# Seven block products for half of an up layer in batch 0's second unit, with its sums in used-up weight columns

## The chip, the cores and the metric

The kernel runs on one core of a Trainium2 chip. The metric is the device time of one execution in microseconds (us), here the median of three runs. One further execution was taken by the hardware profiler; all rows of the trace are from that one.

## The reference

For each of 8 batches, linear attention over 8 heads of 1024 positions and 64 features, and then a maxout layer over the 512 joined features:

```python
k_proj = np.einsum('ks,bhsd->bhkd', E, k)          # 64 rows in place of 1024
v_proj = np.einsum('ks,bhsd->bhkd', F, v)
scores = scale * np.matmul(q, k_proj.transpose(0, 1, 3, 2))
attn = softmax(scores)                              # with its maximum taken off, and 1e-09 added to the sum
x = np.matmul(attn, v_proj)                         # then joined to [8192, 512]
h1 = x @ w1                                         # w1, w2: [512, 1024]
h2 = x @ w2
g = np.maximum(h1, h2)
out = g @ w_out                                     # w_out: [1024, 512]
```

## The kernel before

**The algebra.** With wd = w1 - w2 the layer is max(h1, h2) = relu(x @ wd) + x @ w2, so out = relu(x @ wd) @ w_out + x @ m with m = w2 @ w_out. The first product is called the up layer here, the second sum the down layer. wd_sb and m_sb are made once, on the chip, while batch 0 runs: wd_sb by VectorE in four steps of 256 columns each (`step_wd_rows`, called `wd[0]` to `wd[3]`, two instructions on line 549 each), w2 transposed by TensorE and copied out by ScalarE in four steps (`step_w2t`, lines 557 and 563), and m by `m_steps` (line 634).

**The units.** Each batch has two units of 512 positions; there are 16 units. From batch 1 on, the up layer of a unit is done by block products (`up_steps`): operands are cut in two by two blocks, and seven products of blocks, with sums of blocks made on VectorE before and after, stand in for eight. It is done in two halves d of the feature columns; half d = 1 has the column blocks 2, 3, 6 and 7 of 128 columns each. One product is four matmuls of 256 columns (line 746). The pieces are p1, p2, p6, p5, p7, p3, p4: p1, p6, p5 and p7 are copied out of PSUM by ScalarE (`keep`, line 720), p2 and p3 are added to kept ones by VectorE (line 761), which then takes the relu in place (line 764), and p4 goes out by ScalarE with the relu (line 807). The sums of x that the products need are s_x (`sums_x`, line 706), those of wd are t_w (`step_tw`, line 597); those of g for the down layer are s_g.

**Batch 0** has no such up layer. It takes direct matmuls: `up_slots` gives u0[fb] and u1[fb], for the first and the second unit, fb = 0 to 7, each a block of 128 feature columns by four matmuls of 512 columns (line 525) and a relu out of PSUM, by ScalarE (line 534) except for fb = 3, which VectorE does (line 536). u0[0], u0[1], u1[0] and u1[1] are done in two parts each.

**The order** is written out by hand. `slots` is a list of pieces that all issue in this order; `at_slot` hangs more steps behind a piece. Each engine runs its own instructions in the order in which they were issued, and waits by semaphores for the others. In the stage that the change is in, the list is:

```python
    slots = [
        (0, lambda: u0[0](r0=2)), (1, lambda: u0[1](r0=2)), (None, lambda: loads(1, "v", "q", "k")),
        (None, lambda: step_w2t(256, True)),
        (2, lambda: u1[0](r0=2)), (3, lambda: u1[1](r0=2)),
        (None, wd[1]), (4, u0[2]), (5, u0[3]),
        (None, wd[2]), (6, u1[2]), (7, u1[3]), (None, wt[2]), (None, wt[3]), (8, u0[4]), (9, u0[5]), (None, wd[3]),
        (10, u1[4]), (11, u1[5]), (12, u0[6]), (13, u0[7]),
        (14, u1[6]), (15, u1[7]),
        *((16 + n, x) for n, x in enumerate(m_steps())),
    ]
```

`wt[2]` and `wt[3]` are the transposes of w2's columns from 512 and from 768 on. Behind the pieces of m come those of the down layer of unit 0, `("P", 0, p, i)`.

**Memory.** PSUM has four banks `mm0` to `mm3`, used in turn or by number (`mm_bank`), and two pairs of banks `att` (`att_banks`). s_x, s_g and t_w lie in `big` tiles, which had held E and F (box 0), w1 (box 1), w2 (box 2) and transposed w2 (box 3); `open_box` takes such a tile anew.

Of the kernel before, what the change touches and what calls it, by code (L numbers as in the profile page):

```python
# [19 lines left out]
def kernel(  # L20
# [310 lines left out]
    Z = D // 2  # L331
# [184 lines left out]
    def up_slots(t, j):  # L516
        t["gt", j] = gt = gpool.tile([128, NFB, HALF], FP16, tag="gt", name="gt_sb")
        for fb in range(NFB):
            def up(fb=fb, r0=0, r1=NDC):
                if r0 == 0:  # L520
                    t["up", j, fb] = mm_bank(n=None if r1 == NDC else first_banks[j][fb])
                h_ps = t["up", j, fb]
                order = range(NDC) if fb < 2 else (0, 2, 1, 3)
                for r in order[r0:r1]:
                    nc.tensor.matmul(  # L525
                        out=h_ps,
                        lhsT=wd_sb[:, r, fb * 128 : (fb + 1) * 128],
                        rhs=t["xt"][:, r, :, j * W : (j + 1) * W],
                        start=(r == 0), stop=(r == NDC - 1),
                    )  # L530
                if r1 < NDC:
                    return
                if fb != 3:
                    nc.scalar.activation(out=gt[:, fb, :], in_=h_ps, func=ACTF.Relu)
                else:
                    nc.vector.tensor_scalar_max(gt[:, fb, :], h_ps, 0.0)
            yield up
# [78 lines left out]
    def m_steps():  # L616
# [2 lines left out]

        def product(k, name, n):  # L620
            if n is not None:
                st[name] = mm_bank(n=n)
            bank = st[name]
            Bb = lambda h, c: wo_sb[:, h * NG : (h + 1) * NG, c * CH : (c + 1) * CH]
            T = lambda i: T_sb[:, i, 0:NG, :]
            a, w_ = {
                1: lambda: (m_blk(0, 0), Bb(0, 0)), 2: lambda: (m_blk(0, 1), Bb(1, 0)),
                3: lambda: (m_sums[3], Bb(1, 1)), 4: lambda: (m_blk(1, 1), T(3)),
                5: lambda: (m_sums[0], T(0)), 6: lambda: (m_sums[1], T(1)),
                7: lambda: (m_sums[2], T(2)),  # L630
            }[k]()
            for i in range(2):
                for c in range(NG):
                    nc.tensor.matmul(  # L634
                        out=bank[:, i * CH : (i + 1) * CH],
                        lhsT=a[:, c, i * 128 : (i + 1) * 128],
                        rhs=w_[:, c, :],
                        start=(n is not None and i == 0 and c == 0),
                        stop=(c == NG - 1), skip_group_check=True,
                    )  # L640
            return bank
# [5 lines left out]
            nc.vector.tensor_tensor(out=block(j, c), in0=two(x), in1=two(y), op=ALU.add)  # L647

        def p1():
            st["s1"] = keep("pu", product(1, "X", 2))  # L650

        def p2():
            add(0, 0, product(2, "Y", 3), st["s1"])

        def p6():
            st["u1"] = keep("pu", product(6, "X", None))

        def p5():
            st["s5"] = keep("pu", product(5, "Z", 1))

        def p7():
            st["u2"] = keep("pu", product(7, "X", None))
# [17 lines left out]

    def t_w(i):
        return box[0].rearrange("q (s n m) -> q s n m", s=4, n=NX)[:, i]

    def step_tw(i):
        sub4(
            [t_w(i) for i in range(4)],
            lambda h, c: wd_sb[:, h * NX : (h + 1) * NX, c * HALF : (c + 1) * HALF], (i,),
        )

    def x_blk(u, j, h):  # L690
# [25 lines left out]
        step_s(u, g_blk, s_g, which)  # L716

    def keep(tag, bank, copy=nc.scalar.copy):
        x = ppool.tile([128, 512], FP32, tag=tag, bufs={"pu": 3, "pd": 4}[tag], name="p_sb")
        copy(out=x, in_=bank)  # L720
        return x

    def new_gt(u):
        u["gt"] = gpool.tile([128, NFB, HALF], FP16, tag="gt", name="gt_sb")


    def up_steps(u):
        for d in range(2):
            st = {}
            xbank, ybank = (2, 3) if d == 0 else (3, 2)  # L730

            def product(k, name, n, st=st, d=d):
                if n is not None:
# [21 lines left out]
            two = lambda ap: ap.rearrange("q (m n) -> q m n", m=2)  # L755

            def c_blk(j, c, d=d):
                return u["gt"][:, c * NG + 2 * d : c * NG + 2 * d + 2, j * W : (j + 1) * W]

            def add(j, c, x, y, c_blk=c_blk):  # L760
                nc.vector.tensor_tensor(out=c_blk(j, c), in0=two(x), in1=two(y), op=ALU.add)  # L761
# [1 line left out]
            def relu(ap):  # L763
                nc.vector.tensor_scalar_max(ap, ap, 0.0)  # L764

            def p1(st=st, product=product, xbank=xbank, d=d):
                if d == 0:
                    new_gt(u)
                st["s1"] = keep("pu", product(1, "X", xbank))
# [5 lines left out]
            def p6(st=st, product=product):  # L775
                st["u1"] = keep("pu", product(6, "X", None))

            def p5(st=st, product=product, ybank=ybank):
                st["s5"] = keep("pu", product(5, "Z", ybank))

            def p7(st=st, product=product):
                st["u2"] = keep("pu", product(7, "X", None))
# [230 lines left out]
    def loads(b, *names):  # L1013
        for n in names:
# [12 lines left out]
            elif b_ < B:  # L1027
                load_all(tiles[b_], b_, n, {"k": k, "v": v, "q": q}[n])

    slots = [  # L1030
        (0, lambda: u0[0](r0=2)), (1, lambda: u0[1](r0=2)), (None, lambda: loads(1, "v", "q", "k")),
        (None, lambda: step_w2t(256, True)),
        (2, lambda: u1[0](r0=2)), (3, lambda: u1[1](r0=2)),
        (None, wd[1]), (4, u0[2]), (5, u0[3]),
        (None, wd[2]), (6, u1[2]), (7, u1[3]), (None, wt[2]), (None, wt[3]), (8, u0[4]), (9, u0[5]), (None, wd[3]),
        (10, u1[4]), (11, u1[5]), (12, u0[6]), (13, u0[7]),
        (14, u1[6]), (15, u1[7]),
        *((16 + n, x) for n, x in enumerate(m_steps())),
    ]
    slots = [((0, n), x) for n, x in slots]  # L1040

# [27 lines left out]
        steps.setdefault(key, []).append(lambda: s(*a))  # L1069


    for key, s_, *a in (
        *((10 + i // 2, sums_m, i) for i in range(4)), *((12 + i, step_t, 0, (i,)) for i in range(4)),
        (11, open_box, 1), (11, sums_x, U[0, 0], (0, 1)),
        (15, open_box, 0, 2), (17, sums_x, U[0, 0], (2, 3)),
        (18, sums_g, U[0, 0], (0, 1)), (19, sums_g, U[0, 0], (2, 3)), (22, open_box, 3),
    ):
        at_slot((0, key), s_, *a)


    t = tiles[1]
    at_slot((0, 22), new_attn, t)
    at_slot((0, 22), lambda: turn.__setitem__(slice(None), [2, 3]))
    for n, x in enumerate((
        "", "", "", "", "", "kv", "", "kpt", "qt00 qt10", "", "sc00 sc10", "qt01",
        "qt11 dn00 in00 dn10 in10", "", "", "at00 AT10 sc01",
    )):
        key = ("P", n // 15, (n - 1) // 2 % 7, (n - 1) % 2) if n else (0, 22)
        for name in x.split():
            if name[0] == "k":  # L1090
                if name == "kpt":
# [272 lines left out]
```

## Time and profile before

| | |
|---|---|
| median of 3 runs | 319.89 us (319.75 to 320.46) |
| the profiled execution | 320.29 us |
| its span, first to last instruction | 318.5 us |
| granted TensorE clock | 1.0 |
| TensorE (PE) busy | 311.8 us, 98%, 3922 matmuls |
| VectorE (DVE) busy | 241.1 us, 76% |
| ScalarE (ACT) busy | 206.0 us, 65% |
| GpSimd (POOL) busy | 41.4 us, 13% |

In the rows of the trace the first number is the start in us from the span's start and the second the length; then come the engine, the line of the kernel, the operation, out<-in and the count. PEld is TensorE's weight load. A bracket tells how long the engine was idle before the row and what ended that. Where rows are grouped, the numbers behind the bar are the busy time in us and the mean length of one in ns. Matmuls are pipelined: the length of one is longer than the distance from its start to the next one's.

### The profile page before, as it was taken

To read this page: it belongs to the slowest core of one execution; us is meant where nothing else is said; L and a number is where in the kernel's file an instruction comes from. 1 tells how busy PE (TensorE), PEld (TensorE's weight loads), DVE (VectorE), ACT (ScalarE), POOL (GpSimd) and SP (SyncE) were. 2 spreads that over 40 slices of the span, in tenths; PEclk is the share of its full clock that TensorE was granted. 3 is DMA by queue.
4 is the path that set the end of the run, shared out by engine and by line. 5 is a ranking of instruction groups with operands and counts; after the bars stand their busy time and mean duration, and the time that the engine had idled before them with its cause. 6 is when DMAs were issued, how large, how long until landed. Compare 5 with 4: busy or idle time off the path is not lost.

```text
span 318.5 us, 9309 instructions
## 1 busy us (share of the span) xinstructions
PE 311.8 (98%) x3922; PEld 253.8 (80%) x3922; DVE 241.1 (76%) x442; ACT 206.0 (65%) x373; POOL 41.4 (13%) x63
## 2 busy tenths in 40 slices
PE   7999999999999999999999999999999999999996
PEld 3565588888887888788887888788887888888885
DVE  2366889887969696896969696996969696969883
ACT  2386742777776777477776777477776777765541
POOL 8259102004000300012000400030000000000000
PEclk9999999999999999999999999999999999999999
DMA  7999999999989999799999999989979131313124
GB/s 179 206 202 197 207 207 201 207 156 141 204 163 183 171 209 245 208 188 147 225 229 219 169 199 245 221 155 174 230 153 217 42 101 36 102 35 102 36 99 136
DMA packets 76684, 53.71 MB, mean 169 GB/s; under 512 B 29664, under 2 KB 76128, under 8 KB 76640
## 3 DMA queue, kind: packets, MB, share of 16 engines
q0 software_dynamic: 30688, 28.05, 56.0%
q1 hardware_dynamic: 45664, 24.85, 33.1%
q8 instruction: 31, 0.51, 0.6%
q10 hardware_dynamic: 288, 0.20, 0.2%
q14 instruction: 13, 0.11, 0.1%
HBM read 57.15 MB, written 16.78 MB: 232 GB/s over the span
## 4 chain that ended last, share of the span: by engine, by line
PE 95%; DMA 3%; ACT 1%; DVE 1%; issue 0%; POOLq 0%
PE mm_ps L838 47%; PE mm_ps L746 27%; PE mm_ps L525 4%; PE mm_ps L195 4%; PE att_ps L352 4%; PE mm_ps L340 2%; DMA k_sb<-in_k_dram 2%; PE mm_ps L634 2%; PE att_ps L237 1%; PE mm_ps L311 1%; PE mm_ps L153 1%; DMA out_dram<-o_sb 1%; PE att_ps L340 0%; DVE qt_sb L316 0%; ACT ld_sb L388 0%
## 5 line engine op out<-in xcount | busy, mean ns | idle before, releaser
L720 ACT COPY p_sb<-mm_ps 128x512 f32<-128x512 f32 x179 | 101.7, 592 | 49.2 <-PE mm_ps L746 27.3
L838 PEld LDWEIGHTS <-big 128*128 128x128 f16 x768 | 73.5, 98 | 11.8 <-issue 3.6
L838 PE MATMUL mm_ps<-T_sb,big 128*128 128x256 f16 x576 | 76.9, 273 | 0.0
L761 DVE TENSOR_TENSOR gt_sb<-mm_ps,p_sb 128x512 f16<-128x512 f32 x56 | 38.5, 688 | 43.0 <-PE mm_ps L746 41.6
L746 PE MATMUL mm_ps<-big,big 128*128 128x256 f16 x336 | 50.4, 273 | 0.0
L746 PEld LDWEIGHTS <-big 128*128 128x128 f16 x448 | 43.8, 98 | 5.1
L838 PE MATMUL mm_ps<-wo_sb,gt_sb 128*128 128x256 f16 x256 | 42.6, 273 | 0.0
L838 PEld LDWEIGHTS <-gt_sb 128*128 128x128 f16 x376 | 35.7, 98 | 6.7 <-issue 2.7
L469 ACT ACTIVATE ex_sb<-mm_ps 128x512 f16<-128x512 f32 x50 | 27.2, 597 | 18.0 <-PE mm_ps L340 12.3
L746 PEld LDWEIGHTS <-wd_sb 128*128 128x128 f16 x336 | 32.9, 98 | 3.8
L746 PE MATMUL mm_ps<-xt_sb,wd_sb 128*128 128x256 f16 x224 | 32.8, 273 | 0.0
L499 DVE TENSOR_TENSOR xt_sb<-att_ps,ld_sb 128x1024 f16<-128x1024 f32 x26 | 31.7, 1219 | 0.2
L303 POOL COPY junk<-qt_sb 1x1 f16<-1x1 f16 x6 | 2.6, 432 | 172.3 <-DMA qt_sb<-q_sb 172.3
L838 PE MATMUL mm_ps<-m_sb,xt_sb 128*128 128x256 f16 x128 | 24.4, 273 | 0.0
L869 DVE TENSOR_TENSOR o_sb<-mm_ps,p_sb 128x512 f32<-128x512 f32 x32 | 21.9, 683 | 2.8 <-ACT p_sb L898 2.0
L764 DVE TENSOR_SCALAR gt_sb<-gt_sb 128x512 f16<-128x512 f16 (+1 forms) x60 | 20.9, 348 | 2.1
L706 DVE TENSOR_TENSOR big<-gt_sb 128x1024 f16<-128x1024 f16 x32 | 21.9, 683 | 0.0
L838 PE MATMUL mm_ps<-wo_sb,big 128*128 128x256 f16 x128 | 21.5, 273 | 0.0
L807 ACT ACTIVATE gt_sb<-mm_ps 128x512 f16<-128x512 f32 x28 | 16.8, 601 | 5.7 <-PE mm_ps L746 5.7
L838 PE MATMUL mm_ps<-T_sb,gt_sb 128*128 128x256 f16 x120 | 20.3, 273 | 0.0
L838 PEld LDWEIGHTS <-xt_sb 128*128 128x128 f16 x188 | 18.3, 98 | 2.3 <-issue 0.2
L761 DVE TENSOR_TENSOR gt_sb<-p_sb 128x512 f16<-128x512 f32 x28 | 19.1, 682 | 0.6 <-ACT p_sb L720 0.6
(121 smaller groups left out, 434.8 us busy)
## 6 DMA issues: line engine op xcount, KB each, us to landing
out_dram<-o_sb SPq DMA_DIRECT2D x62, 256.0 KB
k_sb<-in_k_dram POOLq DMA_DIRECT2D x7, 1024.0 KB, 9.7
v_sb<-in_v_dram POOLq DMA_DIRECT2D x7, 1024.0 KB, 15.4
q_sb<-in_q_dram POOLq DMA_DIRECT2D x5, 1024.0 KB, 22.8
q_sb<-in_q_dram POOLq DMA_DIRECT2D x6, 512.0 KB, 15.9
big<-in_moe_w_dram POOLq DMA_DIRECT2D x12, 128.0 KB, 6.4
v_sb<-in_v_dram POOLq DMA_DIRECT2D x4, 256.0 KB, 14.0
wo_sb<-in_moe_w_out_dram POOLq DMA_DIRECT2D x1, 1024.0 KB, 10.4
```

What stands on the lines that cost most here:

```text
L195: nc.tensor.matmul(out=kv_ps[r * KP : (r + 1) * KP, h * D : (h + nh) * D], lhsT=eft[i][:, c, :], rhs=t[w][:, h0 + h : h0 + h + nh, c, :], ...
L352: nc.tensor.matmul(out=dst(r ^ (hh % 2))[hh * Z : (hh + 1) * Z, :], lhsT=weights(rows, hh), rhs=ex[rows, hh % 2, hh // 2 * W : (hh // 2 + ...
L469: nc.scalar.activation(out=t["ex", g, j][:, e, :], in_=banks[e], func=ACTF.Exp, scale=scale)
L499: nc.vector.tensor_tensor(out=x_out(t, g, j).rearrange("q z o n -> q o z n"), in0=at_ps.rearrange("q o (z n) -> q o z n", z=2), in1=ld[:, ...
L706: nc.vector.tensor_tensor(out=S(i), in0=S(0) if x is None else x, in1=y(), op=op)
L720: copy(out=x, in_=bank)
L746: nc.tensor.matmul(out=bank[:, m * W : (m + 1) * W], lhsT=w_[:, n_, (2 * d + m) * 128 : (2 * d + m + 1) * 128], rhs=a[:, n_, :], start=(n ...
L761: nc.vector.tensor_tensor(out=c_blk(j, c), in0=two(x), in1=two(y), op=ALU.add)
L764: nc.vector.tensor_scalar_max(ap, ap, 0.0)
L807: nc.scalar.activation(out=out, in_=in_, func=ACTF.Relu)
L838: nc.tensor.matmul(out=bank[i][:, 0:CH] if two_banks else bank[:, i * CH : (i + 1) * CH], lhsT=a(c)[:, i * 128 : (i + 1) * 128], rhs=w_(c) ...
L869: nc.vector.tensor_tensor(out=o_sb, in0=two(x), in1=two(y), op=ALU.add)
```

## The change

Four direct pieces of batch 0's second unit, u1[2], u1[3], u1[6] and u1[7], are replaced by the d = 1 half of `up_steps`, S1, S2, S6, S5, S7, S3, S4 in the order of issue. The rest of batch 0's up layer stays direct. With it:

- The four sums of xt for unit 1 (`sums_x(U[0, 1], ...)`) are made early, behind wd[1], and before S1. t_w is made in two halves: d = 1 behind wd[3], d = 0 later, during unit 0's down layer.
- s_x of units 0 and 1 (modulo 3) and s_g lie in columns of w1_sb and w2_sb that have been used up, and no longer in boxes of their own.
- All of m's seven products (M1 to M4) go into the `att` banks, and u0 and u1 take turns in `mm0` and `mm1` (by fb modulo 2); S1 to S4 have `mm2` and `mm3`. The transposes of w2 from column 512 and 768 on go into `att` banks too, at other places in the order.
- M2's sum with the kept M1 (`M_add`) is issued later, behind M6 and two sums of g.
- S3's two sums and the relu behind them (`rest`) are held until unit 0's down layer has begun. S1, S6, S5 and S7 are kept in the pool `soft`.

```diff
-                    t["up", j, fb] = mm_bank(n=None if r1 == NDC else first_banks[j][fb])
+                    t["up", j, fb] = mm_bank(n=first_banks[j][fb] if r1 < NDC else fb % 2)
...
             if n is not None:
-                st[name] = mm_bank(n=n)
+                if n % 2 == 0:
+                    st["att"] = att_banks()
+                st[name] = st["att"][:, n % 2, :]
...
         def p2():
-            add(0, 0, product(2, "Y", 3), st["s1"])
+            st["c0"] = product(2, "Y", 1)
...
-        return [p1, p2, p6, p5, p7, p3, p4]
+        return [p1, p2, p6, p5, p7, p3, p4, lambda: add(0, 0, st["c0"], st["s1"])]
 
     def s_g(i):
-        return box[2].rearrange("q (s n m) -> q s n m", s=4, n=NG)[:, i]
+        return (w1_sb, w2_sb)[i // 2][:, :, HALF + i % 2 * CH : HALF + (i % 2 + 1) * CH]
 
     def s_x(i, u):
         n = u["n"] % 3
-        half = box[1 if n < 2 else 3].rearrange("q (h s n m) -> q h s n m", h=2, s=4, n=NX)
-        return half[:, n % 2, i]
+        if n == 2:
+            return box[3].rearrange("q (h s n m) -> q h s n m", h=2, s=4, n=NX)[:, 0, i]
+        r = i % 2 * NX
+        return (w1_sb, w2_sb)[n][:, r : r + NX, i // 2 * CH : (i // 2 + 1) * CH]
...
-    def step_tw(i):
+    def step_tw(i, d):
+        f0 = d * CH
...
-    def up_steps(u):
-        for d in range(2):
+    def up_steps(u, halves=range(2)):
+        for d in halves:
             st = {}
-            xbank, ybank = (2, 3) if d == 0 else (3, 2)
+            tag = "soft" if u["b"] == 0 else "pu"
+            xbank, ybank = (2, 3) if d == 0 or u["b"] == 0 else (3, 2)
...
                 bank = product(3, "Z", None)
+                if u["b"] == 0:
+                    def rest(u=u, st=st, d=d, bank=bank):
+                        add(0, 1, bank, st["u1"])
+                        add(1, 1, st["u2"], st["s5"])
+                        relu(up_gt(u)[:, NG + 2 * d : NG + 2 * d + 2, :])
+
+                    u["rest"] = rest
+                    return
...
+    open_box(0)
+    S1, S2, S6, S5, S7, S3, S4 = up_steps(U[0, 1], (1,))
+    M1, M2, M6, M5, M7, M3, M4, M_add = m_steps()
     slots = [
-        (0, lambda: u0[0](r0=2)), (1, lambda: u0[1](r0=2)), (None, lambda: loads(1, "v", "q", "k")),
...
+        lambda: u0[0](r0=2), lambda: u0[1](r0=2), lambda: loads(1, "v", "q", "k"),
+        lambda: step_w2t(256, True),
+        lambda: u1[0](r0=2), lambda: u1[1](r0=2), wd[1], lambda: sums_x(U[0, 1], range(4)),
+        u0[2], u0[3], S1, S2, lambda: step_w2t(512, True), wd[2],
+        u0[4], lambda: step_w2t(768, True), u0[5], wd[3], lambda: [step_tw(i, 1) for i in range(4)] and None,
+        u1[4], S6, u1[5], S5, u0[6], S7, u0[7],
+        lambda: [sums_m(i) for i in range(4)] and None, S3, S4,
+        lambda: step_t(0, (0, 1)), M1, lambda: step_t(0, (2, 3)), M2, lambda: sums_x(U[0, 0], (0, 1)),
+        M6, lambda: sums_g(U[0, 0], (0, 1)), M_add, M5, lambda: sums_g(U[0, 0], (2, 3)), M7, M3, M4,
+        lambda: (open_box(3), new_attn(tiles[1]), turn.__setitem__(slice(None), [2, 3])) and None,
     ]
...
-        if n in (2, 3):
-            for i in range(2):
-                at_slot(key, step_tw, 2 * (n - 2) + i)
+        if n == 2:
+            at_slot(key, sums_x, U[0, 0], (2, 3))
+        if n == 3:
+            at_slot(key, lambda: U[0, 1]["rest"]())
         if 6 <= n < 10:
-            at_slot(key, sums_x, U[0, 1], ((2, 0, 1, 3)[n - 6],))
+            at_slot(key, step_tw, n - 6, 0)
```

In the changed kernel the lines stand lower: the products of `m_steps` are on line 636, `keep` copies on 728, `up_steps` multiplies on 758, adds on 773, takes its relu in place on 776 and p4's on 827, the sums s_x and s_g are on 711, and the down layer multiplies on 858 (838 before).

More of the change, by code (lines that the diff above doesn't have):

```diff
@@ L718, in keep, with up_gt @@
     def keep(tag, bank, copy=nc.scalar.copy):
-        x = ppool.tile([128, 512], FP32, tag=tag, bufs={"pu": 3, "pd": 4}[tag], name="p_sb")
+        if tag == "soft":
+            x = soft.tile([128, 512], FP32, tag=tag, name="p_sb")
+        else:
+            x = ppool.tile([128, 512], FP32, tag=tag, bufs={"pu": 3, "pd": 4}[tag], name="p_sb")
         copy(out=x, in_=bank)
         return x
+    def up_gt(u):
+        return u["t"]["gt", u["o"]] if u["b"] == 0 else u["gt"]
     def new_gt(u):
         u["gt"] = gpool.tile([128, NFB, HALF], FP16, tag="gt", name="gt_sb")
-    def up_steps(u):
-        for d in range(2):
+    def up_steps(u, halves=range(2)):
+        for d in halves:
             st = {}
-            xbank, ybank = (2, 3) if d == 0 else (3, 2)
+            tag = "soft" if u["b"] == 0 else "pu"
+            xbank, ybank = (2, 3) if d == 0 or u["b"] == 0 else (3, 2)
             def product(k, name, n, st=st, d=d):
@@ L757, in c_blk @@
             def c_blk(j, c, d=d):
[L758 removed]
+                return up_gt(u)[:, c * NG + 2 * d : c * NG + 2 * d + 2, j * W : (j + 1) * W]
             def add(j, c, x, y, c_blk=c_blk):
@@ L1087 @@
     )):
-        key = ("P", n // 15, (n - 1) // 2 % 7, (n - 1) % 2) if n else (0, 22)
+        key = ("P", n // 15, (n - 1) // 2 % 7, (n - 1) % 2)
         for name in x.split():
```

42 lines of the change are left out of this document (13 added, 29 removed).

## The prediction

> **What bounds the kernel now.** I read the page's busy times and its chain first, then TensorE's list of waits, then busy times by window, and last the timelines of TensorE, VectorE and ScalarE from 24 to 46 us, where the change lies.
>
> ```profile
> span 318.5 us, 9309 instructions
> PE 311.8 (98%) x3922; PEld 253.8 (80%) x3922; DVE 241.1 (76%) x442; ACT 206.0 (65%) x373; POOL 41.4 (13%) x63
> PE 95%; DMA 3%; ACT 1%; DVE 1%; issue 0%; POOLq 0%
> ```
>
> TensorE works 311.8 of 318.5 us, and the chain that ends last is TensorE for 95% of its length. Where the other 6.7 us lie is told by its waits, longest first, and by one window:
>
> ```profile
> PE mm_ps L153 <- DVE ones L146: 1.5, 1, 1.5
> PE mm_ps L1196 <- DMA out_dram<-o_sb: 1.2, 1, 1.2
> PE mm_ps L195 <- DMA k_sb<-in_k_dram: 1.0, 1, 1.0
> PE att_ps L352 <- ACT vp_sb L207: 0.5, 1, 0.5
> ...
> 24.00:64.00 40.00, 40.00 (x464) 28.86 (x462) 32.38 (x63) 23.42 (x39) 10.54 (x14) 1.00 1.29 204
> ```
>
> The list has seven waits in all, and by their lines they belong to the start, to the attention of batch 0 and to the last store. In the window the columns are length, then busy time of PE, weight loads, DVE, ACT and POOL: TensorE is busy for 40.00 of 40.00 us. So in the stage that the change rewrites TensorE has no slack. A microsecond of its work taken out is worth a microsecond; a microsecond for which it is made to wait costs one, and nothing later gives it back, as no wait follows until the last store.
>
> **The work taken out of TensorE.** Its timeline through the stage, and the length of one matmul:
>
> ```profile
> 27.31 4.48 PE L525 MATMUL mm_ps<-xt_sb,wd_sb 128*128 128x512 f16 x20
> 31.63 1.06 PE L557 MATMUL mm_ps<-ident,big 128*128 128x128 f16 x16
> 32.52 7.07 PE L525 MATMUL mm_ps<-xt_sb,wd_sb 128*128 128x512 f16 x32
> 39.43 1.91 PE L634 MATMUL mm_ps<-wo_sb,big 128*128 128x256 f16 x16
> 41.17 2.78 PE L634 MATMUL mm_ps<-T_sb,p_sb 128*128 128x256 f16 x24
> L525 PE MATMUL mm_ps<-xt_sb,wd_sb 128*128 128x512 f16 x64 | 14.5, 379 | 0.0
> L746 PE MATMUL mm_ps<-big,big 128*128 128x256 f16 x336 | 50.4, 273 | 0.0
> ```
>
> Start to start gives the price in the stream: (39.43 - 32.52) / 32 = 0.216 us for 512 columns, (41.17 - 39.43) / 16 = 0.109 for 256, (32.52 - 31.63) / 16 = 0.0556 for a transpose. The change drops four pieces of the second unit (u1[2], u1[3], u1[6], u1[7]: 16 matmuls of 512 columns, 3.45 us) and adds seven products of four matmuls of 256 columns (28 x 0.109 = 3.05 us). That is a gain of **0.40 us** and no more: 0.13% of the time, too small to be told from no change here (about 0.2%, or 0.64 us, is what can be told). Whatever the rest of the change does, its price is weighed against these 0.40 us.
>
> **The wait that is put in.** The new order on TensorE from u0[3] on is: u0[3], S1, S2, eight transposes of w2, u0[4]. u0[4] reads the columns of wd_sb that step wd[2] makes on VectorE. VectorE runs its queue in order, and there wd[2] now stands behind two new instructions: S2's sum with the kept S1 (line 773), and a relu of that sum (line 776). Before, wd[2] stood directly behind the relu of u0[3]. The rows of before:
>
> ```profile
> 27.22 0.42 DVE L549 TENSOR_TENSOR wd_sb<-big,big 128x512 f16<-128x512 f16 x1 [0.25 <-DMA big<-in_moe_w_dram]
> 30.10 0.69 DVE L536 TENSOR_SCALAR gt_sb<-mm_ps 128x512 f16<-128x512 f32 x1 [2.46 <-PE mm_ps L525]
> 30.71 0.84 DVE L549 TENSOR_TENSOR wd_sb<-big,big 128x512 f16<-128x512 f16 x2
> 31.83 0.69 DVE L536 TENSOR_SCALAR gt_sb<-mm_ps 128x512 f16<-128x512 f32 x1 [0.28 <-PE mm_ps L525]
> 32.44 0.75 DVE L549 TENSOR_TENSOR wd_sb<-big,big 128x512 f16<-128x512 f16 x2
> 34.23 0.69 DVE L706 TENSOR_TENSOR p_sb<-big 128x1024 f16<-128x1024 f16 x1 [1.05 <-ACT big L563]
> 28.97 1.62 ACT L534 ACTIVATE gt_sb<-mm_ps 128x512 f16<-128x512 f32 x3
> 32.27 1.93 ACT L563 COPY big<-mm_ps 128x1024 f16<-128x1024 f16 x2 [0.71 <-PE mm_ps L557]
> 40.50 0.58 ACT L720 COPY p_sb<-mm_ps 128x512 f32<-128x512 f32 x1 [0.28 <-PE mm_ps L634]
> ```
>
> Before, wd[2] was done at 30.71 + 0.84 = 31.55, and u0[4] started at 32.52: a cover of one microsecond. Now the two sides run like this.
>
> TensorE: u0[3]'s last matmul still starts at 27.31 + 11 x 0.216 = 29.69 and ends 0.38 later, at 30.07 (VectorE starts on it at 30.10, so 0.03 to 0.04 after an end). S1 starts at 29.90 and ends at 29.90 + 3 x 0.109 + 0.27 = 30.50. S2 starts at 30.34 and ends at 30.94. The transposes start at 30.77, and after 8 x 0.0556 TensorE is free for u0[4] at **31.22**.
>
> ScalarE keeps S1: behind its relus, which end at 30.59 and overlap the next start a little, and 0.04 after S1's end, so from 30.54; 0.58 long, done at 31.12. VectorE follows ScalarE by 0.03 (32.27 + 1.93 = 34.20, and its row starts at 34.23), so the sum starts at 31.15. What follows such a sum, in a later up layer of the same form:
>
> ```profile
> 83.84 0.69 DVE L761 TENSOR_TENSOR gt_sb<-mm_ps,p_sb 128x512 f16<-128x512 f32 x1 [0.42 <-PE mm_ps L746]
> 84.56 0.29 DVE L764 TENSOR_SCALAR gt_sb<-gt_sb 128x512 f16<-128x512 f16 x1
> 84.77 0.68 DVE L869 TENSOR_TENSOR o_sb<-mm_ps,p_sb 128x512 f32<-128x512 f32 x1
> 12.11 1.29 DVE L316 COPY qt_sb<-mm_ps 128x1024 f16<-128x1024 f16 x2 [0.90 <-PE mm_ps L311]
> 13.45 0.41 PE L340 MATMUL att_ps<-qt_sb,kpt_sb 64*32 64x256 f16 x16 [0.16 <-DVE qt_sb L316]
> ```
>
> The relu starts 0.72 after the sum (31.87), and the next independent instruction 0.21 after that: wd[2]'s first half at 32.08, 0.42 long (line 549's rows), done at 32.50. TensorE follows VectorE by 0.05 (12.11 + 1.29 = 13.40, then 13.45). So u0[4] starts at 32.55 and not at 31.22: a stall of **1.33 us**. wd[2]'s second half comes 0.33 later (two take 0.75, one 0.42), at 32.83, and is wanted at 32.55 + 2 x 0.216 = 32.98, so it adds nothing.
>
> From there to the first matmul of w2 @ w_out TensorE has 24 x 0.216 + 20 x 0.109 + 8 x 0.0556 = 7.81 us: 40.36 against 39.43 before, **0.93 us later**. That is the 1.33 less the 0.40.
>
> Bounds. Below: if ScalarE were no hindrance, the sum would start at 30.98, as S2 itself ends at 30.94, and the net is +0.75. Above: if wd[2] waited for the relu's end (0.29 and not 0.21), and TensorE followed VectorE as late as it did here,
>
> ```profile
> 23.37 0.48 DVE L541 TENSOR_TENSOR wd_sb<-big,big 128x256 f16<-128x256 f16 x2
> L541 DVE TENSOR_TENSOR wd_sb<-big,big 128x256 f16<-128x256 f16 x2 | 0.5, 283 | 0.0
> 23.82 1.41 PEld L525 LDWEIGHTS <-wd_sb 128*128 128x128 f16 x8 [0.21 <-DVE wd_sb L541]
> ```
>
> where the first piece of wd_sb was done at 23.37 + 0.28 = 23.65 and its weights were loaded at 23.82, 0.17 later and not 0.05, the net is +1.13. I take 0.93, as each of its steps has a row of the same engines and shape.
>
> **What is moved and costs nothing.** The four sums of xt go into VectorE's idle time ahead of u0[3]'s relu: from 27.67, four of about 0.42 with two that depend on each other, done by 29.3, against 30.10. Should they run on, they would delay that relu and with it all of the above. The shared operands t_w for S6 come after wd[3]: about 33.6 to 35.2, S6 wants them at 32.55 + 4 x 0.216 + 0.45 + 8 x 0.216 = 35.6, and it is the second of the four, done at 34.5, that it reads. The four sums for w2 @ w_out wait for the last copy of transposed w2 (about 35.1) and end near 37.8; then the T products wait for w_out:
>
> ```profile
> 27.03 0.88 POOL L143 DMA_DIRECT2D wo_sb<-in_moe_w_out_dram  x1
> wo_sb<-in_moe_w_out_dram POOLq DMA_DIRECT2D x1, 1024.0 KB, 10.4
> ```
>
> It lands at 27.03 + 10.4 = 37.4, three microseconds ahead of its use by M1 at 40.4. The second of the T products is done near 39.2 and is read by M6 at 42.1. The other banks for w2 @ w_out have been free since the last transposes were copied. M_add, put behind two sums, is done near 43.1; its block is read by the first piece of the down layer only after 46.5. The held sums and relu of S3 take the places on VectorE in which t_w was made before, and t_w's other half takes the places of the sums of xt; they are read units later. No DMA moves in its queue, on POOL or SP. The slot that issues loads waits for TensorE at the same point, so batch 2's loads slip by the same 0.9 us as their readers.
>
> **The rivals.** *The gain is kept.* Slower turns into not slower if wd[2] is done by 31.17, so that TensorE meets it: then 319.89 - 0.40 = 319.49. For it: only that the chain's end-to-start gaps are worked out and not seen. Against it: S2 must end before its sum starts, and 30.98 + 0.72 + 0.21 + 0.42 is 32.33 with nothing else in the way. Chance 0.08.
>
> *The delay is absorbed.* If a later wait that the profile doesn't show had slack, the time would stay near 319.9. The full window and the list of waits speak against it. Chance 0.10.
>
> *The banks.* u0 and u1 now take turns in two banks, where four were used, so u1[4] needs ScalarE's relu of u0[4] to be over, and u1[5] that of u0[5], behind a 1 us copy of transposed w2. By the rows above these relus end near 34.2 and 35.6, wanted at 34.7 and 36.0: margins of 0.5 and 0.4. If ScalarE ran later by a whole relu, 0.6 each, the stall would grow by some 0.1 to 0.2 each; if it fell behind by a whole copy (1.0), by 0.5 each, thus 321.8. Chance 0.06.
>
> *The clock.* At its start TensorE runs at half speed, and a short stop later doesn't bring that back:
>
> ```profile
> 1.47 3.43 PE L153 MATMUL mm_ps<-ones 128*128 128x512 f16 x8 [1.47 <-DVE ones L146]
> 8.57 1.03 PE L195 MATMUL mm_ps<-k_sb,eft 128*64 128x256 f16 x8 [1.04 <-DMA k_sb<-in_k_dram]
> ```
>
> The first eight matmuls of 512 columns come every (3.43 - 0.38) / 7 = 0.44 us, twice the 0.216 of later. After the stop of 1.04 us at 8.57 eight of 256 columns come every (1.03 - 0.27) / 7 = 0.109, which is full speed. The new stall is 1.33, a little longer than any stop shown but the first. If it did throw TensorE back for as long as the first stretch, eight matmuls would lose 0.21 each, 1.7 us: 322.5. Chance 0.02. The Trainium skill, "TensorE: Matmul & The Clock Gate", Part 1, says that the clock halves after one idle window of about 3.4 us and needs as long a busy one to return; by that rule a stall of 1.33 us is free of it, and the row at 8.57 agrees as far as 1.04 us goes.
>
> **How the numbers follow.** The profiled execution took 320.29 us for its span of 318.5; the median of the three runs is 319.89 (319.75 to 320.46). The difference, +0.93, goes on the median: 320.82, which I give as 320.8 (the span would be 319.4). The forecast has chance 0.74; its own range, with its bounds and the 0.3 us or so by which runs differ, is 320.4 to 321.3. The range down to 320.2 and up to 321.6 takes in some of the absorbed case and of the banks, and leaves out under 2 in 10. Slower by over 0.2% (above 320.53): 0.68 of the forecast, and the banks and the clock, 0.76. Within 0.2%: 0.06 of the forecast, 0.10 of absorption, 0.05 of the kept gain, 0.21. Faster by over 0.2%: TensorE's work allows only 0.40 us, so it is what runs may scatter, 0.03.
>
> **What would show it.** In the profile of the changed kernel: a wait of TensorE on line 525 put down to VectorE's wd_sb (line 549), 1.1 to 1.5 us long, near 31.2 to 32.6; ahead of it on VectorE the rows of lines 773, 776 and 549 in that order, the first starting near 31.15 and released by ScalarE; the first matmul of line 636 near 40.4; no other TensorE wait up to 315 us. The prediction is wrong if TensorE passes from line 557 to line 525 there without a wait, if line 549's third instruction is done before 31.5, or if the matmuls behind the stall come slower than one in 0.216 us.

## The result, and the profile after

| | before | changed |
|---|---|---|
| median, 5 runs each | 319.75 us (319.63 to 320.46) | 323.32 us (323.14 to 323.65) |
| the profiled execution, its span | 320.29, 318.5 | 323.32, 321.5 |
| granted TensorE clock | 1.0 | 1.0 |

By the medians the changed kernel takes 3.57 us more; the ratio over all runs is 1.0108, with a 95% interval of 1.0096 to 1.0119. Slower was forecast, but 320.8, with a range up to 321.6.

The head of the page of the changed kernel, and its window from 24 to 64 us (length, then busy time of PE, weight loads, DVE, ACT, POOL):

```profile
span 321.5 us, 9348 instructions
PE 312.0 (97%) x3934; PEld 255.0 (79%) x3934; DVE 244.3 (76%) x450; ACT 207.0 (64%) x375; POOL 39.7 (12%) x63
...
24.00:64.00 40.00, 37.56 (x421) 28.18 (x420) 32.30 (x67) 23.27 (x39) 10.30 (x13) 1.00 1.29 204
```

TensorE's busy time grew by only 0.2 us, so the loss is waiting: in the window that was full before, 2.44 us are idle now. The first six of the ten rows of TensorE's waits in the changed kernel (total, times, longest):

```profile
PE mm_ps L153 <- DVE ones L146: 1.5, 1, 1.5
PE mm_ps L1211 <- DMA out_dram<-o_sb: 1.5, 1, 1.5
PE mm_ps L525 <- DVE wd_sb L549: 1.2, 1, 1.2
PE att_ps L636 <- ACT p_sb L728: 0.7, 1, 0.7
PE mm_ps L195 <- DMA k_sb<-in_k_dram: 0.6, 1, 0.6
PE att_ps L636 <- DVE m_sb L649: 0.5, 1, 0.5
```

The third row is the wait that was forecast. The two on line 636, in w2 @ w_out, were not. The second is the wait of the program's last matmul (the gate, which waits for a store); it was 1.2 before. TensorE's timeline shows where the three waits stand:

```profile
26.89 2.75 PE L525 MATMUL mm_ps<-xt_sb,wd_sb 128*128 128x512 f16 x12
29.48 1.04 PE L758 MATMUL mm_ps<-xt_sb,wd_sb 128*128 128x256 f16 x8
30.35 0.61 PE L557 MATMUL att_ps<-ident,big 128*128 128x128 f16 x8
32.20 1.04 PE L525 MATMUL mm_ps<-xt_sb,wd_sb 128*128 128x512 f16 x4 [1.24 <-DVE wd_sb L549]
...
40.02 1.04 PE L636 MATMUL att_ps<-wo_sb,big 128*128 128x256 f16 x8
41.73 1.03 PE L636 MATMUL att_ps<-wo_sb,big 128*128 128x256 f16 x8 [0.67 <-ACT p_sb L728]
42.60 1.91 PE L636 MATMUL att_ps<-T_sb,p_sb 128*128 128x256 f16 x16
45.03 1.03 PE L636 MATMUL att_ps<-T_sb,p_sb 128*128 128x256 f16 x8 [0.53 <-DVE m_sb L649]
...
47.65 0.38 PE L858 MATMUL mm_ps<-wo_sb,gt_sb 128*128 128x256 f16 x2
```

A wait costs more than its bracket says: the bracket counts from the end of the matmul before, and that matmul is 0.27 us long where the next one would have started 0.109 after it. Start to start, less the matmuls in between at the prediction's prices: u0[4] loses 32.20 - 30.35 - 8 x 0.0556 = 1.41, M2 loses 41.73 - 40.02 - 8 x 0.109 = 0.84, M7 loses 45.03 - 42.60 - 16 x 0.109 = 0.69. That is 2.94, less the 0.40 of work saved: 2.54.

Every profiled span can be cut at three matmuls: the first of the up layer (23.82 before), the first of the down layer (line 838 before, 858 after), and the last before the gate. The third part is 269.67 us in every kernel below (269.68 in one), so nothing that happens in batch 0 is given back or made worse later. What is left is the start, the stage with the change, and the tail from the start of that last down-layer matmul to the span's end:

| kernel | start | stage | tail | median us |
|---|---|---|---|---|
| before | 23.82 | 21.72 | 3.31 | 319.75 |
| changed | 23.39 | 24.26 | 4.17 | 323.32 |

Stage +2.54, tail +0.86, start -0.43: 2.97, the difference of the two spans. The start moves from execution to execution, from 23.09 (b1) to 24.12 (a9) in the profiles below; the chain of the kernel before leads there through the transfer of k, that of the changed kernel through the transfer of v. The profiled execution of before took 0.54 over its median, the changed kernel's took its median; so the medians differ by 3.57 where these two executions differ by 3.03.

### The profile page after: what moved, and what is told of

The parts are those of the page before. It is cut to its first block, busy times and chain, and to the rows that moved or that the text cites. A ratio compares the mean times of both kernels' runs of the same rounds, so it can differ in the third digit from the quotient of the medians.

```text
span 321.5 us, 9348 instructions
## 1 busy us (share of the span) xinstructions
PE 312.0 (97%) x3934; PEld 255.0 (79%) x3934; DVE 244.3 (76%) x450; ACT 207.0 (64%) x375; POOL 39.7 (12%) x63
## 4 chain that ended last, share of the span: by engine, by line
PE 89%; DMA 5%; ACT 3%; POOL 1%; DVE 1%; issue 0%; POOLq 0%; DVEq 0%
PE mm_ps L858 46%; PE mm_ps L758 27%; DMA v_sb<-in_v_dram 4%; PE att_ps L352 3%; PE mm_ps L195 3%; PE mm_ps L340 2%; PE mm_ps L525 2%; PE att_ps L636 2%; PE att_ps L237 1%; ACT gt_sb L534 1%; DMA out_dram<-o_sb 1%; ACT big L563 1%; PE mm_ps L311 1%; ACT p_sb L728 1%; POOL k_sb L108 0%; POOL q_sb L108 0%
## 5 line engine op out<-in xcount | busy, mean ns | idle before, releaser
L858 PEld LDWEIGHTS <-big 128*128 128x128 f16 x768 | 73.5, 98 | 11.8 <-issue 3.6
L773 DVE TENSOR_TENSOR gt_sb<-mm_ps,p_sb 128x512 f16<-128x512 f32 x58 | 39.9, 687 | 42.7 <-PE mm_ps L758 40.9
L758 PE MATMUL mm_ps<-big,big 128*128 128x256 f16 x348 | 52.2, 273 | 0.0
L758 PEld LDWEIGHTS <-big 128*128 128x128 f16 x464 | 45.4, 98 | 5.9
L758 PEld LDWEIGHTS <-wd_sb 128*128 128x128 f16 x348 | 34.1, 98 | 4.4
L758 PE MATMUL mm_ps<-xt_sb,wd_sb 128*128 128x256 f16 x232 | 33.8, 273 | 0.0
L776 DVE TENSOR_SCALAR gt_sb<-gt_sb 128x512 f16<-128x512 f16 (+1 forms) x62 | 22.1, 357 | 2.1
L303 POOL COPY junk<-qt_sb 1x1 f16<-1x1 f16 x6 | 1.7, 276 | 168.7 <-DMA qt_sb<-q_sb 168.7
```

What stands on the lines that cost most here:

```text
L758: nc.tensor.matmul(out=bank[:, m * W : (m + 1) * W], lhsT=w_[:, n_, (2 * d + m) * 128 : (2 * d + m + 1) * 128], rhs=a[:, n_, :], start=(n ...
L858: nc.tensor.matmul(out=bank[i][:, 0:CH] if two_banks else bank[:, i * CH : (i + 1) * CH], lhsT=a(c)[:, i * 128 : (i + 1) * 128], rhs=w_(c) ...
```

## The experiments

All were run in five rounds beside the kernel before on the same chip; its medians there were 319.82 (for a1, a2, b1 and b2), 319.98 (a5 to a7), 319.87 (b3, a8, b4) and 320.07 (a9, a10). Theory: three TensorE waits, each with its own cause in the order or in the banks, and a tail that depends on the length of the instruction streams. Rivals: the waits overlap so that taking one away only lengthens the next; the tail is chance, or follows from the stage.

**M2's product in a bank of its own tile (a1).** In the changed kernel X and Y, the results of M1 and M2, are the two banks of one `att` tile. Here Y goes into `mm0`.

```diff
-                if n % 2 == 0:
-                    st["att"] = att_banks()
-                st[name] = st["att"][:, n % 2, :]
+                st[name] = mm_bank(n=0) if name == "Y" else att_banks()[:, 0, :]
```

> The changed kernel, with M2's bank (Y) taken from mm0, so that X and Y of w2 @ w_out no longer share one two-bank tile; nothing else. Theory of the shared tile: M2's wait for ScalarE's copy of M1 (0.67 us shown, 0.84 of start-to-start) and M7's wait for M_add (0.53 shown, 0.68) both go, and the time falls by 1.5 us, to about 321.8. Rival, ScalarE or VectorE simply being late there: the two waits stay, the time stays at 323.3.

Measured: 321.9 us, ratio 1.0061 [1.0048, 1.0074]; stage 22.82. TensorE's timeline of this kernel through w2 @ w_out:

```profile
40.47 1.04 PE L634 MATMUL att_ps<-wo_sb,big 128*128 128x256 f16 x8
41.34 1.04 PE L634 MATMUL mm_ps<-wo_sb,big 128*128 128x256 f16 x8
42.21 2.78 PE L634 MATMUL att_ps<-T_sb,p_sb 128*128 128x256 f16 x24
44.83 1.04 PE L634 MATMUL att_ps<-wo_sb,p_sb 128*128 128x256 f16 x8
```

M2 follows M1 by 0.87 us and M7 stands in an unbroken row of 24: both waits are gone with the shared tile, and the only TensorE wait left between 24 and 315 us is that on wd[2]. VectorE's sum of M2 and M1, which stands at the same place in the order, starts here before ScalarE has begun to copy M6 (42.48 against 43.29), and in the changed kernel only behind that copy.

**wd[2] ahead of S1 and S2 (a2).**

```diff
-        u0[2], u0[3], S1, S2, lambda: step_w2t(512, True), wd[2],
+        u0[2], u0[3], wd[2], S1, S2, lambda: step_w2t(512, True),
```

> The changed kernel, with wd[2] issued ahead of S1 and S2, so that on VectorE it stands ahead of S2's sum and relu; nothing else. Theory of the queue: TensorE's wait at u0[4] (1.24 us shown, 1.40 of start-to-start) goes, and the time falls by 1.2 to 1.4 us, to about 322.0. Rival, wd[2] waits for its weights from memory: the wait only shrinks, and VectorE's wd[2] shows a wait on a transfer; the time falls by under 0.7 us.

Measured: 322.51, ratio 1.0077 [1.0064, 1.009]; stage 23.45, which is 0.81 less than the changed kernel's and not 1.41. TensorE still loses 0.28 ahead of u0[4]'s third matmul and 0.30 ahead of S6, start to start. VectorE's timeline of this kernel tells why:

```profile
30.25 0.42 DVE L549 TENSOR_TENSOR wd_sb<-big,big 128x512 f16<-128x512 f16 x1
30.99 0.42 DVE L549 TENSOR_TENSOR wd_sb<-big,big 128x512 f16<-128x512 f16 x1 [0.32 <-DMA big<-in_moe_w_dram]
31.34 0.69 DVE L773 TENSOR_TENSOR gt_sb<-mm_ps,p_sb 128x512 f16<-128x512 f32 x1
32.06 0.70 DVE L776 TENSOR_SCALAR gt_sb<-gt_sb 128x512 f16<-128x512 f16 x1
32.67 0.74 DVE L549 TENSOR_TENSOR wd_sb<-big,big 128x512 f16<-128x512 f16 x2
33.45 0.42 DVE L597 TENSOR_TENSOR big<-wd_sb 128x512 f16<-128x512 f16 x1
```

wd[2]'s second half now finds that its weights have only just landed, and the sum and relu of S2 stand in front of wd[3] and t_w instead, for which S6 waits. So the two VectorE instructions cost TensorE time in both orders, 1.41 and 0.30, as in both an operand that it needs soon is queued behind them.

**Before, with w2 @ w_out in the shared tiles alone (b2).** The changed kernel's `m_steps` and `M_add` behind M6, and nothing else of the change.

```diff
-                st[name] = mm_bank(n=n)
+                if n % 2 == 0:
+                    st["att"] = att_banks()
+                st[name] = st["att"][:, n % 2, :]
...
```

> The kernel before, with the products of w2 @ w_out put into the two pairs of att banks and M2's sum issued behind M6 and two sums of g, as the change does; the up layer is as before. Theory of the shared tile: two waits of TensorE on line 636 or so, 1.5 us of start-to-start in all, 321.3 in all, and no longer tail, as TensorE has as many instructions as before. Rival, the waits need the up layer's new work on ScalarE and VectorE: no such waits, within 0.3 us of the kernel before.

Measured: 321.5, ratio 1.0049 [1.0037, 1.0061]; stage 23.24, that is +1.52; tail 3.31. Its TensorE waits between 24 and 315 us are these two:

```profile
PE att_ps L636 <- ACT p_sb L722: 0.7, 1, 0.7
PE att_ps L636 <- DVE m_sb L649: 0.5, 1, 0.5
```

With a1 this shows the shared tile from both sides.

**Before, with 24 more TensorE instructions (b1).** Twelve one-column matmuls on ones, each with its weight load, in the start's wait for the first transfers.

```diff
+    w_ps = mm_bank()
+    for _ in range(12):
+        nc.tensor.matmul(
+            out=w_ps[0:1, 0:1], lhsT=ones16[:, 0:1], rhs=ones16[:, 0:1], start=True, stop=True
+        )
+    turn.insert(0, turn.pop())
```

> The kernel before, with twelve matmuls of one column added in TensorE's idle time near 7.5 us, 24 instructions of TensorE, as many as the change adds in all; nothing else. Theory of the fetch: a 16 KB fetch of TensorE's instructions that came after the last stores now comes on top of them, SyncE's issues of the last stores lengthen, and the time rises by 0.6 to 1.2 us, to about 320.7, all of it behind the last matmul of the last down layer. Rival, the tail's lengthening comes from another part of the change or from chance: the time stays within 0.3 us of the kernel before.

Measured: 323.33, ratio 1.0109 [1.0095, 1.0124]: as much as the loss of the whole change, where 320.7 was expected, with a stage of 21.87. The profiled execution is the fastest of the four, 322.42; its loss is in the tail, 6.00 against 3.31, and the 0.9 us more of the median was not profiled. The last store is done when it was before (1.94 behind the last down-layer matmul, 1.93 before). SyncE, which ends the program, waits there for TensorE's sequencer:

```profile
SPq L1365 <- PEq L1212: 2.8, 1, 2.8
```

and the DMA's queues from 315 us on show one 16 KB fetch of instructions more (packets, MB, share); in this kernel

```profile
q8 instruction: 2, 0.03, 2.3%
```

against, in the kernel before,

```profile
q8 instruction: 1, 0.02, 1.1%
```

So the end of this program is not indifferent to how many instructions ran before it. But this is not the changed kernel's tail: there TensorE's last but one 16 KB fetch starts 1.38 us ahead of the last down-layer matmul, here 2.50 behind it, and the branch with which TensorE's program ends takes 0.49 us there, 3.38 here and 0.38 in the kernel before.

**The changed kernel with twelve fewer fill-in matmuls (a5)**, which gives TensorE's stream its old length: `warm(3)` and four of the five `warm(2)` of batch 0's start become `mm_bank()`, the fifth `warm(1)`.

> The changed kernel with twelve fewer warm-up matmuls in TensorE's idle time before 18 us (24 instructions fewer, so that TensorE's program is as long as before the change); the banks take turns as they did. Theory of the fetch: the stretch from the last matmul of the down layer to the end of the span falls from 4.2 to the 3.3 us of before, the three waits of the stage stay, and the time falls by about 0.9 us, to 322.4. Rival, the long tail comes from where the change put things in memory or from the late end itself: the tail stays at 4.0 or more and the time at 323.3.

Measured: 323.28, ratio 1.0102 [1.0088, 1.0117], not the 322.4 of the theory. TensorE's additional fetch ahead of the gate was gone, but the tail only went from 4.17 to 3.92, and in this profile the start was later by 0.23 and the stage longer by 0.09.

**All three waits out (a6):** a1, the fewer fill-in matmuls, wd[2] ahead of S1, and S2's sum and relu put behind t_w.

```diff
-                add(0, 0, product(2, "Y", ybank), st["s1"])
-                relu(c_blk(0, 0))
+                bank = product(2, "Y", ybank)
+                def first(st=st, bank=bank):
+                    add(0, 0, bank, st["s1"])
+                    relu(c_blk(0, 0))
+
+                if u["b"] == 0:
+                    u["first"] = first
+                    return
+                first()
...
-        u0[4], lambda: step_w2t(768, True), u0[5], wd[3], lambda: [step_tw(i, 1) for i in range(4)] and None,
+        u0[4], lambda: step_w2t(768, True), u0[5], wd[3], lambda: [step_tw(i, 1) for i in range(4)] and None, lambda: U[0, 1]["first"](),
```

> The changed kernel with its own bank for M2, wd[2] ahead of S1, S2's sum and relu behind the four t_w sums on VectorE, and twelve fewer warm-up matmuls. By the theories all of the waits but one go: u0[4]'s third matmul still waits about 0.3 us for the second half of wd[2], whose weights land then. The block products' gain of 0.40 less 0.3 is left: 319.7, within 0.2% of the kernel before. Rival, a delayed S2 sum makes a new wait for bank mm3 at S5 or at M6's sums: a wait on line 758 or 636 and 320.2 or more.

Measured: 320.5, ratio 1.0009 [0.999, 1.0027], where 319.7 was expected; stage 21.65, tail 3.90. The tail's 0.59 over that of before had not been counted. The stage beats the one of before by 0.07; a gap of 0.28 for the landing of wd[2]'s second weights remains. **a7** splits w2's load from column 512 on in two so that those weights land sooner:

```diff
-        (w2_sb, moe_w2, 256, 512), (w1_sb, moe_w1, 256, 512), (w2_sb, moe_w2, 512, DF),
-        (w1_sb, moe_w1, 512, 768), (w1_sb, moe_w1, 768, DF),
+        (w2_sb, moe_w2, 256, 512), (w1_sb, moe_w1, 256, 512), (w2_sb, moe_w2, 512, 768),
+        (w1_sb, moe_w1, 512, 768), (w2_sb, moe_w2, 768, DF), (w1_sb, moe_w1, 768, DF),
```

> As the one before, and with w2's columns 512 to 1023 loaded in two halves, columns 512 to 767 of w2 and w1 first, so that wd[2] has its weights 1.2 us sooner; two more loads on GpSimd's queue. By the theories no wait of TensorE is left between 24 and 315 us, and the block products' gain of 0.40 shows: 319.4, 0.1% below the kernel before. Rival, the two extra issues delay w_out or batch 1's loads enough to make a later wait: the time is at or above 319.8, with a wait on a transfer on line 636 or 237.

Measured: 320.53, ratio 1.0019 [1.0006, 1.0031]. The profiled run (320.02) has no gap at all: stage 21.33, tail 3.30. Its up layer also starts 0.74 later than a6's (23.95 against 23.21), which gives the weights more time; but a8 below, with the same loads, has no gap ahead of u0[4]'s third matmul either and starts at 23.41. So the 0.40 us of saved matmuls are real (21.72 - 21.33 = 0.39). Yet the runs spread from 319.72 to 321.64, with six of the twelve at 320.76 or more, and the median gained nothing. Why is open; the loads are the only difference from a6.

**What the tail hangs on (b3, a8, b4).** b3 is before with the fewer fill-in matmuls of a5; a8 is a7 with all of them; b4 is before with more instructions on VectorE and ScalarE:

```diff
     nc.vector.tensor_copy(out=ident16, in_=ident)
+    for i in range(11):
+        nc.vector.memset(junk, 0.0)
+    for i in range(4):
+        nc.scalar.copy(out=junk, in_=ones16[0:1, 0:1])
```

> The kernel before with twelve of the start's fill-in matmuls on ones left out (24 TensorE instructions fewer), which the versions with the rearranged stage also leave out. Theory (a program's end depends on where the last fetches of instructions fall; the fill-in matmuls themselves stand in waits and cost nothing): the stage is the one of before, the fetch that stood behind the gate matmul comes no earlier, 319.6 to 320.2. Rival (leaving the fill-in out costs something at the start, a later start of the up layer or a lower granted clock): 320.3 to 320.8, and the up layer's first matmul of the second unit comes 0.3 to 0.8 us later than 23.82.

> The version without any TensorE wait in the stage (separate banks, late sum, split loads) with all of the fill-in matmuls back, so 24 TensorE instructions longer than before, as the changed kernel is. Theory (the longer program brings a 16 KB fetch of TensorE's instructions ahead of the gate and among the last stores): the tail from the last matmul of the down layer to the end of the span is 3.9 to 4.5 us where it was 3.3, and the time 320.9 to 321.5. Rival (TensorE's length has no part in it): tail 3.3, time 319.6 to 320.5 as without the fill-in.

> The kernel before with eleven one-element memsets on VectorE and four one-element copies on ScalarE at the start, in their wait for the first transfers, which is as many instructions as the changed kernel has more on these two engines. Nothing in the stage moves. Theory (the 8 KB fetches of instructions near the end belong to one of these engines, and come earlier and among the last stores when its program is longer): the tail is 3.7 to 3.9 us where it was 3.3, time 320.3 to 320.6. Rival (their length has no part in it): tail 3.3, 319.7 to 320.2.

Measured: b3 319.9, ratio 1.0006 [0.9997, 1.0015], stage 21.72, tail 3.31: the fill-in is free. b4 320.61, ratio 1.0032 [1.002, 1.0044], stage 21.72, tail 3.91: +0.60 from fifteen more instructions of VectorE and ScalarE at the start, with the stage untouched. a8 320.61, ratio 1.0029 [1.0017, 1.0042], tail 3.49, stage 21.84: TensorE's longer program puts 0.2 on the tail where 0.6 to 1.2 were expected; the stage is 0.5 longer than a7's, 0.42 of it from a wait of w2 @ w_out's last product on ScalarE that a7 did not have.

In b4's DMA list from 0.5 to 2.0 us behind the last down-layer matmul stands a fetch of instructions among the last stores (q1 and q10):

```profile
q1 hardware_dynamic: 286, 0.19, 43.7%
q10 hardware_dynamic: 263, 0.18, 39.1%
q14 instruction: 1, 0.01, 1.4%
```

In the same stretch of the kernel before there is none:

```profile
q1 hardware_dynamic: 296, 0.20, 42.9%
q10 hardware_dynamic: 271, 0.18, 39.1%
```

Sorted by where that 8 KB fetch starts, from the last down-layer matmul, with the end of the last store:

| | 8 KB fetch | last store done | tail |
|---|---|---|---|
| before, b2, b3 | +2.17 to +2.22 | 1.93 to 1.95 | 3.31 |
| a7 | -1.15 | 1.94 | 3.30 |
| a8, with TensorE's longer program | -1.15 | 2.03 | 3.49 |
| b4, a5, a6 | +1.05 or +1.06 | 2.42 or 2.43 | 3.90 to 3.92 |
| a1, a2, changed, with TensorE's longer program | +1.02, +0.72, +0.72 | 2.52, 2.90, 2.68 | 3.97, 4.47, 4.17 |

Where it stands before the last stores or after them, these land when they did before or 0.1 later; where it stands among them, they land half a microsecond later or more, and the gate and the end wait for them.

**Three and four instructions more, to move that fetch (a9, a10).** If this is so, a longer program can be a faster one. a9 is a6, a10 the changed kernel, with one-element memsets on VectorE in b4's place, three and four of them.

> The version with separate banks, the late sum and the shortened fill-in (320.5, its tail 3.90 us with an 8 KB fetch of instructions 1.05 us after the last matmul of the down layer), and three one-element memsets more on VectorE at the start, in its wait for the first transfers. Theory (that fetch belongs to VectorE's program and falls a fixed number of its instructions from the start, so three more instructions bring it ahead of the last stores, as it stands at 1.15 us ahead of that matmul in the version with split loads): tail 3.3, time 319.8 to 320.1, less with more instructions. Rival (the tail of 3.90 comes from the rearranged stage or by chance): tail 3.9, 320.4 to 320.7.

> The changed kernel with four one-element memsets more on VectorE at the start. The stage with its three waits is not touched. Theory: the 8 KB fetch moves from 0.72 us behind the last matmul of the down layer to about 1.1 us ahead of it, the tail shrinks from 4.17 to 3.5 us and the time from 323.3 to 322.5 to 322.8. Rival (the position of that fetch has no part in it): tail 4.1 to 4.2, 323.1 to 323.6.

Measured: a9 319.94, ratio 0.9995 [0.9979, 1.0011], where a6 had 320.5: the fetch stands at -1.18, the last store is done at 1.93, and the tail is 3.31. Its stage, 21.33, has no gap, but not through the memsets: in this profile the up layer starts at 24.12, 0.91 later than in a6, and by then the weights have landed. The tail's 0.59 is enough for the 0.56 between the two medians. a10 322.92, a little above the range expected, ratio 1.0082 [1.0065, 1.0098]: the fetch at -1.19, tail 3.54 in place of 4.17, its stage 24.26 as in the changed kernel. The gate's wait alone does not tell the two cases apart; in a9, in a10 and in b4 it is:

```profile
PE mm_ps L1218 <- DMA out_dram<-o_sb: 1.2, 1, 1.2
```

```profile
PE mm_ps L1213 <- DMA out_dram<-o_sb: 1.4, 1, 1.4
```

```profile
PE mm_ps L1200 <- DMA out_dram<-o_sb: 1.5, 1, 1.5
```

a10's gate waits nearly as long as b4's, though its tail is 0.37 shorter; the end of the last store (2.03 against 2.43) is the better sign. a9 is the best version of the change that was found, and it can't be told from the kernel before.

The traces say a little more of that fetch. Its place goes with VectorE's program: counted in VectorE's records of the trace, it starts behind the 575th to 581st in every version that has 585 or more of them, and the versions with 573 or 574 (before, b1, b2, b3) have no such fetch until behind the last stores. And the stores are late in more ways than one. In b4 and a5 they are issued when they were before, within 0.07, and their last packets come late. In a1 and a6 VectorE's third sum from the end starts 0.37 later (0.01 behind the last down-layer matmul, -0.36 before), ahead of the fetch and with nothing that its semaphores show to wait for. In the changed kernel and a2 SyncE's issues take longer: the one at -1.14 takes 1.29 and 1.26 us where it took 0.42, the last one 0.83 and 1.06 where it took 0.36. So the fetch's place tells whether the tail is long; that the fetch itself holds the stores up is not shown for all of these versions.

## Why the prediction was right and where it was wrong

**What bounds the kernel: right.** TensorE's stream is the time. A stall in the stage is never given back: 269.67 us from the down layer to the end in every kernel. This also settles the rival that the delay is absorbed.

**The work taken out: right.** 0.40 us was worked out; 0.39 shows as soon as no wait stands in the stage (a7, a9).

**The wait that is put in: right.** This profile's stage runs 0.42 us earlier than the one of before (26.89 against 27.31). With that taken off the forecast's times, S2's sum was to start at 30.73, released by ScalarE, and u0[4] at 32.13. VectorE's timeline of the changed kernel:

```profile
30.73 0.69 DVE L773 TENSOR_TENSOR gt_sb<-mm_ps,p_sb 128x512 f16<-128x512 f32 x1 [0.36 <-ACT p_sb L728]
31.46 0.35 DVE L776 TENSOR_SCALAR gt_sb<-gt_sb 128x512 f16<-128x512 f16 x1
31.73 1.41 DVE L549 TENSOR_TENSOR wd_sb<-big,big 128x512 f16<-128x512 f16 x4
...
44.29 0.69 DVE L649 TENSOR_TENSOR m_sb<-att_ps,p_sb 128x512 f16<-128x512 f32 x1 [2.21 <-ACT p_sb L728]
```

The sum starts at 30.73, u0[4] at 32.20, M1 at 40.02 against 39.94. Up to there the net loss was forecast as 0.93 and is 1.01; in a2, with the order turned round, u0[4] starts without a wait.

**"What is moved and costs nothing": the step that failed.** It said of the banks for w2 @ w_out that they "have been free since the last transposes were copied", and of M_add that it is "done near 43.1". Free at M1's start they were, as M1 starts without a wait; what was not asked is who reads them between the products. M1's and M2's results lie in one two-bank tile. M2 therefore waits until ScalarE has copied M1 out, although M2 writes the other bank (0.84 lost), and M7, which goes on in M1's bank, waits until M_add has read M2's (0.69). M_add itself only started at 44.29: the last row above, which the trace puts down to ScalarE's copy of M6 from the tile's other bank. Together 1.53, shown by b2 (+1.52 alone) and by a1 (both gone). In a1 and in the changed kernel alike M1's and M2's results lie in two different banks; only the tile differs, and the wait goes with it. Whether an earlier M_add would have spared M7 its wait in the shared tile was not tried. The Trainium skill, "PSUM — Partial Sum Buffer", section "PSUM bank collisions raise a hardware error", names the bank and the quadrant of its partitions as what engines must not share at one time; by that rule M1's and M2's separate banks need no wait on each other, and in a1, where they lie in separate tiles, there is none. The prediction's rival on "the banks" went by `mm0` and `mm1` of the up layer, where no wait appeared, and not by the tiles of w2 @ w_out.

**The tail was not a term of the sum at all.** The step counted instructions only by the time they take. The change adds 24 instructions to TensorE's stream and 15 to those of VectorE and ScalarE, and the tail grew by 0.86: b4 gives 0.60 for the 15 by themselves, and with the 8 KB fetch moved away (a10) 0.23 is left, near the 0.19 that TensorE's longer program costs in a8 against a7. The gate matmul in the kernel before carries the reason "a fetch of instructions waits for a store" in its code; the prediction passed over it.

The sum that would have held is 1.01 + 1.53 + 0.86 = 3.40 against the measured 3.57; the rest, 0.17, is within what the starts of executions differ (23.09 to 24.12 in these profiles).

**The other rivals.** The gain was not kept, as the wait came. The clock did not fall: behind the stop of 1.24 us the four matmuls of u0[4] come every (1.04 - 0.38) / 3 = 0.22 us, and the granted clock is 1.0 throughout, which agrees with the rule of the Trainium skill, "TensorE: Matmul & The Clock Gate", Part 1, that was quoted for it.

## What to carry to other kernels

When results move into other PSUM banks, follow each tile through its readers as well as its owner: two banks in one tile are waited for together, and a chain product, copy, product becomes serial where it was pipelined. On an engine that runs in order, a sum put in front of an urgent operand holds that operand up for its whole end-to-start path (1.41 us of TensorE's time here), and moving it behind only helps if nothing urgent follows it there either (0.30 in a2). Where a change of a few tenths is weighed, look at the program's last microseconds in each profile: here three or four instructions at the program's start moved them by 0.6 us.

## What the runs showed of the hardware that was not expected

Twelve one-column matmuls at the start cost 3.5 us (b1), and four one-element memsets took 0.63 us off a tail (a10). The traces show fetches of 16 KB (queue 8, whose number rises from 31 to 32 with TensorE's 24 more instructions) and of 8 KB (queue 14) between the data transfers. The Trainium skill, "Runtime: NRT & Kernel Launch", section "Instruction fetch mechanics", says that engines fetch their programs in blocks by their own DMA queues, at a cost that is mostly hidden. That holds here up to the last stores: the 269.67 us from the down layer on are the same in every version, wherever the fetches fall. It does not hold at the end: the tail with an 8 KB fetch among the last stores was 0.6 us longer (b4). In b1 2.7 us were lost behind the gate, where TensorE's sequencer took 3.38 us for its branch at the program's end, 0.38 before. A 16 KB fetch falls within that branch, but the kernel before has one at nearly the same place (2.54) behind a short branch, and the one that b1 has more starts only after the branch has ended; that the branch waits for a fetch is a guess, and was not tried. The fetch on queue 14 that moved is VectorE's as far as a9 and a10 tell, which lengthened VectorE's program alone; whether that queue also carries the programs of other engines was not separated.
